# A chunked-attention and gated-FFN kernel: its hand-written order and its engine letters replaced by another set

## The chip, the cores and the metric

The kernel runs on one core of a Trainium2 chip. The metric is device time in microseconds (us) of one execution, on the core that ends last (here the only one). Smaller is better.

## The reference

Attention in chunks of 32 queries, each with 16 keys to the left, 8 to the right and 8 memory keys, then a feed-forward block with a depthwise convolution that makes its own gate. The sizes are batch 4, 8 heads, 768 tokens, head width 64, so a model width of 512, and an inner width of 1024. All inputs but q, k, v and the memory come as float64 words.

```python
for c in range(nc):                       # 24 chunks of 32 queries
    k_full = concat(mem_k, k[l_start:r_end])      # 16 left, 32, 8 right, 8 memory
    scores = scale * q_c @ k_full.T
    a = exp(scores - max); a = a / (sum(a) + 1e-9)
    out[c] = a @ v_full
x = out as (B, S, 512)
h = maximum(x @ w_in, 0)                  # (B, S, 1024)
conv = sum_k conv_w[k] * shift(h, k)      # 3 taps over the tokens
y = (h * sigmoid(conv)) @ w_out
```

## The kernel before

The work is cut into 1309 small operations, each a Python closure that emits a few instructions. A plan records, for each, which tiles it reads and writes; `Plan.run` then emits them in the sequence of the table `ORDER` (lines 35 to 91). Each engine (PE, DVE, ACT, POOL) and the queue of the loads (SP) executes its own instructions strictly in that sequence, so a waiting instruction holds back all behind it on its engine. Strings of letters choose an engine or a variant for each piece: `SOFT` the softmax of a step, `NORM` the engine of its division, `W_IN` and `W_OUT` the way a float64 weight block is taken apart, `TAP`, `MULT` and `LO` the engines of the gate.

The text uses these names for the operations:

- **Steps 0 to 31** are pieces of the attention: one batch, one half of the tokens, two heads each; steps 0 to 3 are done one at a time, later ones in pairs named by the first. qN, kN and vN are the three loads of step N (line 301; on SP, 192, 252 and 384 KB). **S N** is the scores of step N on PE (line 310: 48 weight loads and 48 matmuls in the trace); **T N** the transposes of its probabilities (line 325); **V N** the product with v (line 334).
- The softmax between S and T: maximum (DVE, line 267), then for letter V a subtraction on DVE (line 269) and one exponential on ACT (line 270), for letter A a scaling of the maximum by a negative number on DVE (line 272) and on ACT, straight from PSUM, one exponential for each of 6 (single step) or 12 (pair) slices (line 283); then the sum (290), the reciprocal (293) and the division (294, on DVE or POOL). The score tile `s` is there once: S of the next step waits until the softmax has read it.
- After T, ACT copies the transposed tile (`w_t`, 327), V runs, ACT rounds its result (`x_hi`, 340) and DVE takes the rest (`x_lo`, 341). The tile `t` is there once as well, so the next T waits for that `x_lo`.
- **in0 to in7, out0 to out7** are the loads of the float64 blocks of w_in and w_out (line 208, 512 KB each) and the DVE, ACT and POOL operations that split each into two fp32r parts (lines 212 to 238).
- **F** is a group of three matmuls of 128x384 (line 358), one block of w_in times one quarter of x; **O** a group of three of 128x512 (line 402) for the output. In the whole program there are 256 F, 200 O, 32 S, 18 T and 18 V.

SP's loads go through eight lanes: a load's issue waits until the load eight places ahead of it has landed, and, where its buffer is in use, for the engine that still reads it.

```python
W_IN, W_OUT = ('CSSRMSCr', 'CMCRRSRM')
SOFT = 'VVVVVAAVVAVBVVVBVBVVVAVVVVAVVBAA'
...
            assert after <= done, i
...
        e = Tile('e', lambda: e_of[len(plan.rings['e'][1]) % len(e_of)])
...
    plan.run(ORDER)
```

Of the kernel before, what the change touches and what calls it, by code (L numbers as in the profile page):

```python
# [24 lines left out]
W_IN, W_OUT = ('CSSRMSCr', 'CMCRRSRM')  # L25
TAP = 'AAAAAAAAVAVAVVVAVAVAVVAAVVAAVVAV'
MULT = 'VVVGVVGVVVVVGGGVGVVVVGVVVGGGVVVV'
LO = 'VVVVGGGVVVVVVVVVGVVVGVVVVGVVGVGV'
SOFT = 'VVVVVAAVVAVBVVVBVBVVVAVVVVAVVBAA'
NORM = 'GGVGGGVVGGGGGVGGVVGGVVVVVVVGVGVG'  # L30
# [71 lines left out]
class Plan:  # L102

    def __init__(self):
        self.ops, self.last, self.readers = ([], {}, defaultdict(list))
        self.rings, self.parts = ({}, defaultdict(list))
# [434 lines left out]
```

## Time and profile before

| | |
|---|---|
| median of 3 runs | 353.03 us (352.73 to 353.37) |
| the profiled execution | 352.37 us |
| its span | 350.6 us |
| instructions | 10290 |
| PE, DVE, ACT, POOL busy | 334.1, 233.1, 191.9, 83.6 us |
| HBM read, written | 35.55 MB, 6.29 MB |

The span runs from the first to the last recorded instruction; 1.77 us of the profiled execution's time lie around it. Busy times of different engines overlap, so they do not add up to the span. A busy PE is not a PE at its peak: matmul records overlap one another, and where the next one starts tells the pace better than how long one lasts.

### The profile page before, as it was taken

The page shows a single profiled execution, that of the slowest core. Times are in us where ns is not written, and L with a number is a line of the kernel's source. Part 1 is how long each engine was busy: PE and PEld are TensorE (multiplying, and loading weights), DVE is VectorE, ACT ScalarE, POOL GpSimd, SP SyncE. Part 2 cuts the span into 40 slices and gives each one's busy share as a digit, 9 for nine tenths or more (in the row PEclk, how much of TensorE's full clock was granted, in tenths as well). Part 3 has the DMA queues.
Part 4 walks back from the last instruction along what each step waited for, and adds up shares of the span by engine and source line. Part 5 has one row for each costly group of instructions (what it writes and reads, how often), then busy time and mean ns, then how long its engine had stood idle before and what let it go on. Part 6 is the DMA issues. An engine that isn't in the chain of part 4 may idle for free.

```text
span 350.6 us, 10290 instructions
## 1 busy us (share of the span) xinstructions
PE 334.1 (95%) x4536; PEld 297.1 (85%) x4536; DVE 233.1 (66%) x325; ACT 191.9 (55%) x314; POOL 83.6 (24%) x127
## 2 busy tenths in 40 slices
PE   1589999999999999999999999999999999999996
PEld 0468999989999998887888999998888988998885
DVE  4977998999989997989974143286840332678300
ACT  4434785877687869379842323456743352545311
POOL 1464245124473154111020000402200012121200
PEclk9999999999999999999999999999999999999999
DMA  7966979667677244022401600001212000100022
GB/s 261 391 216 204 314 249 333 230 208 228 200 206 251 66 154 148 27 93 75 125 20 36 243 0 32 0 2 60 65 45 93 30 1 2 60 0 2 0 105 76
DMA packets 19916, 42.49 MB, mean 121 GB/s; under 512 B 2336, under 2 KB 10784, under 8 KB 19872
## 3 DMA queue, kind: packets, MB, share of 16 engines
q1 hardware_dynamic: 19872, 41.85, 35.6%
q8 instruction: 35, 0.57, 0.7%
q14 instruction: 9, 0.07, 0.1%
HBM read 35.55 MB, written 6.29 MB: 119 GB/s over the span
## 4 chain that ended last, share of the span: by engine, by line
PE 85%; DVE 9%; DMA 3%; issue 1%; ACT 0%; POOL 0%; DVEq 0%; ACTq 0%; POOLq 0%
PE f L402 38%; PE f L358 34%; PE t L334 6%; PE s L310 4%; PE t L325 3%; DMA w<-in_w_out_dram 2%; DVE c L378 1%; DMA w<-in_w_in_dram 1%; DVE w_top L217 1%; DVE e L269 1%; DVE top L267 1%; DVE w_top L214 1%; DVE w L223 1%; DVE w_top L216 1%; DVE w L221 1%
## 5 line engine op out<-in xcount | busy, mean ns | idle before, releaser
L402 PE MATMUL f<-w_out_hi,g 128*128 128x512 f32 (+1 forms) x400 | 127.3, 387 | 0.0
L358 PE MATMUL f<-x_hi,w_in_hi 128*128 128x384 f32 x256 | 90.3, 353 | 0.0
L402 PEld LDWEIGHTS f<-w_out_hi,g 128*128 128x128 f32 x400 | 74.1, 188 | 15.2 <-ACT o_sb L405 0.2
L358 PE MATMUL f<-x_lo,w_in_hi 128*128 128x384 f32 x256 | 86.7, 339 | 0.0
L358 PE MATMUL f<-x_hi,w_in_lo 128*128 128x384 f32 x256 | 86.7, 339 | 0.0
L402 PE MATMUL f<-w_out_lo,g 128*128 128x512 f32 (+1 forms) x200 | 77.0, 385 | 0.0
L378 DVE SCALAR_TENSOR_TENSOR c<-h,cw,c 128x768 f32<-128x768 f32 x48 | 49.2, 1044 | 18.6 <-ACT c L374 17.4
L358 PEld LDWEIGHTS f<-x_hi,w_in_hi 128*128 128x128 f32 x256 | 48.6, 190 | 2.7 <-issue 0.2
L358 PEld LDWEIGHTS f<-x_hi,w_in_lo 128*128 128x128 f32 x256 | 48.8, 190 | 1.0
L358 PEld LDWEIGHTS f<-x_lo,w_in_hi 128*128 128x128 f32 x256 | 48.5, 190 | 0.0
L402 PEld LDWEIGHTS f<-w_out_lo,g 128*128 128x128 f32 x200 | 37.6, 188 | 6.6
L405 ACT COPY o_sb<-f 128x512 f32<-128x512 f32 (+1 forms) x25 | 14.2, 573 | 43.4 <-PE f L402 41.3
L379 ACT ACTIVATE c<-c 128x768 f32<-128x768 f32 x32 | 26.9, 847 | 19.6 <-DVE c L378 19.5
L366 ACT ACTIVATE h<-f 128x384 f32<-128x384 f32 x48 | 22.6, 490 | 26.3 <-PE f L358 26.3
L388 POOL TENSOR_TENSOR g<-c,g 128x768 fp32r<-128x768 f32 x8 | 15.4, 1925 | 70.9 <-PE f L402 35.2
L334 PEld LDWEIGHTS t<-w_t,v_t 64*64 64x64 f32 x1536 | 25.2, 140 | 4.6 <-issue 3.3
L334 PE MATMUL t<-w_t,v_t 64*64 64x32 f32 x1536 | 27.2, 224 | 0.1
L387 ACT CAST g<-c 128x768 fp32r<-128x768 f32 x24 | 19.8, 833 | 12.6 <-POOL c L381 7.1
L376 DVE TENSOR_SCALAR c<-h,cw 128x768 f32<-128x768 f32 x14 | 8.6, 617 | 26.3 <-ACT h L366 23.6
L388 DVE TENSOR_TENSOR g<-c,g 128x768 fp32r<-128x768 f32 x16 | 17.3, 1086 | 11.2 <-ACT g L387 11.0
L381 POOL TENSOR_TENSOR c<-c,h 128x768 f32<-128x768 f32 x5 | 8.9, 1781 | 63.4 <-ACT c L379 63.4
L341 DVE TENSOR_TENSOR x_lo<-t,x_hi 128x768 fp32r<-128x768 f32 (+1 forms) x18 | 15.5, 859 | 12.6 <-ACT x_hi L340 12.6
(68 smaller groups left out, 408.5 us busy)
## 6 DMA issues: line engine op xcount, KB each, us to landing
v_t<-in_v_dram SPq DMA_DIRECT2D x32, 384.0 KB, 4.4
k_t<-in_k_dram SPq DMA_DIRECT2D x28, 252.0 KB, 3.9
out_dram<-o_sb SPq DMA_DIRECT2D x23, 256.0 KB, 2.0
q_d<-in_q_dram SPq DMA_DIRECT2D x28, 192.0 KB, 4.4
w<-in_w_in_dram SPq DMA_DIRECT2D x8, 512.0 KB, 6.2
w<-in_w_out_dram SPq DMA_DIRECT2D x8, 512.0 KB, 5.3
h<-in_k_dram SPq DMA_DIRECT2D x4, 252.0 KB, 6.1
h<-in_q_dram SPq DMA_DIRECT2D x4, 192.0 KB, 5.8
```

Source lines behind the costliest of these rows:

```text
L310: nc.tensor.matmul(s.t[w * CH:(w + 1) * CH, h ^ w & 1, (i * NG + g) * KW:(i * NG + g + 1) * KW], lhsT=q_d.t[r, c], rhs=k_t.t[r, c * STEP:c ...
L325: nc.tensor.transpose(out=t.t[:, j, g * P:(g + 1) * P], in_=e.t[:, i, 1:1 + 2 * KW], identity=ident)
L334: nc.tensor.matmul(t.t[h * D:(h + 1) * D, c & 1, c // 2 * CH:(c // 2 + 1) * CH], lhsT=vs[i].t[r, o], rhs=w_t.t[r, i, o], start=True, stop= ...
L341: plan.op(lambda: nc.vector.tensor_tensor(out=lo(), in0=sums(), in1=hi().bitcast(F32), op=ALU.subtract), (t, *keys(x_hi)), keys(x_lo))
L358: nc.tensor.matmul(f.t[:, :TW], lhsT=w_in_p[c][:, fc, cc], rhs=x_p[a].t[:, cc], start=cc == 0 and i == 0, stop=cc == NCC - 1 and i == 2)
L366: nc.scalar.activation(h.t[:, 1 + o:1 + o + TW], f.t[:, :TW], AF.Relu)
L378: plan.op(lambda i=i: nc.vector.scalar_tensor_tensor(out=c.t, in0=h.t[:, i:i + S], scalar=w[i], in1=c.t, op0=ALU.mult, op1=ALU.add), (*H, ...
L379: plan.op(lambda: nc.scalar.activation(c.t, c.t, AF.Sigmoid), (c,), (c,))
L387: plan.op(lambda: nc.scalar.copy(out=g_hi(), in_=x()), (h,), (p[0],))
L388: plan.op(lambda: (nc.vector if lo == 'V' else nc.gpsimd).tensor_tensor(out=g_lo(), in0=x(), in1=g_hi().bitcast(F32), op=ALU.subtract), (h ...
L402: nc.tensor.matmul(ps.t[:, :n], lhsT=g[fc][a].t[:, tt * P:(tt + 1) * P], rhs=w_out_p[c][:, fc, o:o + n], start=fc == 0 and i == 0, stop=fc ...
L405: plan.op(lambda: nc.scalar.copy(out=o_sb.t[:, :n], in_=ps.t[:, :n]), (ps,), (o_sb,))
```

## The change

The table `ORDER` is replaced as a whole (1308 entries now), with the letters that go with it. The way the two probability buffers `e` are handed out is changed too: no longer in turn, but whichever has been given back first; and the check that a ring has a free buffer counts the buffers in use.

```diff
-W_IN, W_OUT = ('CSSRMSCr', 'CMCRRSRM')
-TAP = 'AAAAAAAAVAVAVVVAVAVAVVAAVVAAVVAV'
-MULT = 'VVVGVVGVVVVVGGGVGVVVVGVVVGGGVVVV'
-LO = 'VVVVGGGVVVVVVVVVGVVVGVVVVGVVGVGV'
-SOFT = 'VVVVVAAVVAVBVVVBVBVVVAVVVVAVVBAA'
-NORM = 'GGVGGGVVGGGGGVGGVVGGVVVVVVVGVGVG'
+W_IN, W_OUT = ('CSSSCRmR', 'SMCSRRSC')
+TAP = 'AAAAAAAAAAAVVAAVVVAAVVVAAAAAAAVV'
+MULT = 'VVVGGVVVVGGVGGVGGVVVGGVGGVGGGGVV'
+LO = 'VVVVVVVVVVVVVVGGGGGGVGVVVGGGVVGG'
+SOFT = 'AAVVVAVVVAABAVVBVBVVVAVVVVVVVBVA'
+NORM = 'GGVGGGGVVGGGVVVGGVGGVVVVGVGGGGGG'
 ORDER = (
-    64, 65, 1, 0, 3, 75, 17, 16, 85, 70, 33, 32, 66, 67, 18, 68, 69, 2, 71, 72, 73, 74, 4, 76, 190, 49, 5, 6, 19, 77,
+    64, 0, 1, 75, 16, 17, 85, 70, 65, 33, 71, 48, 2, 66, 73, 67, 68, 72, 69, 32, 3, 74, 4, 18, 76, 5, 49, 6, 77, 95,
...
-                    assert len(used) < size or not used[-size].left, i
+                    assert sum((y.left > 0 for y in used)) < size, i
...
             do()
+            for x in tiles:
+                if not x.left and x.ring in self.freed:
+                    self.freed[x.ring].append(x.t)
...
+    plan.ring('e', len(e_of))
+    plan.freed['e'] = e_of
...
-        plan.ring('e', len(e_of))
-        e = Tile('e', lambda: e_of[len(plan.rings['e'][1]) % len(e_of)])
+        e = Tile('e', lambda: plan.freed['e'].pop(0))
```

Four lines are added ahead of these pieces, so a line of the new kernel has a number larger by 3 to 5 than before (line 310 is 314 now, 358 is 362). In both orders in0 is the first load. The program has as many S, T, V, F and O as before.

**SP, the loads 10 to 22.** Before, in this sequence: v1 and v0, q4, k3, q5, q3, q6, k4, in3, k5, v3 and v2, in4, k6.

```order
L301 DMA v_t<-in_v_dram 128x768 x2
L301 DMA q_d<-in_q_dram 128x384
L301 DMA h<-in_k_dram 128x504
L301 DMA q_d<-in_q_dram 128x384
L301 DMA h<-in_q_dram 128x384
L301 DMA q_d<-in_q_dram 128x384
L301 DMA k_t<-in_k_dram 128x504
L208 DMA w_228<-in_w_in_dram 128x1024
L301 DMA k_t<-in_k_dram 128x504
L301 DMA v_t<-in_v_dram 128x768 x2
L208 DMA w_353<-in_w_in_dram 128x1024
L301 DMA k_t<-in_k_dram 128x504
```

Now, behind q3 and v0: q2, v1, k3, in3, v2, k5, v3, q5 and q4, k4, q6, v5, in4.

```order
L305 DMA h<-in_q_dram 128x384
L305 DMA v_t<-in_v_dram 128x768
L305 DMA h<-in_k_dram 128x504
L213 DMA w_154<-in_w_in_dram 128x1024
L305 DMA v_t<-in_v_dram 128x768
L305 DMA k_t<-in_k_dram 128x504
L305 DMA v_t<-in_v_dram 128x768
L305 DMA q_d<-in_q_dram 128x384 x2
L305 DMA k_t<-in_k_dram 128x504
L305 DMA q_d<-in_q_dram 128x384
L305 DMA v_t<-in_v_dram 128x768
L213 DMA w_368<-in_w_in_dram 128x1024
```

in3 and two of the large v loads have moved ahead of the q and k of step 4; in4 stands behind v5, whose buffer is free only after V1, where before it stood behind a v that waits for V0.

**PE, from S3 on.** Before: S3, V1, the first F, S5 and S4 together, the second F, T2.

```order
L310 MATMUL s<-h 32x64 x24
L334 MATMUL t<-w_t,v_t 64x32 x24
L358 MATMUL f<-x_hi_270,w_in_hi 128x384
L358 MATMUL f<-x_hi_270,w_in_lo 128x384
L358 MATMUL f<-x_lo_273,w_in_hi 128x384
L310 MATMUL s<-k_t,q_d 32x64 x48
L358 MATMUL f<-x_hi_270,w_in_hi 128x384
L358 MATMUL f<-x_hi_270,w_in_lo 128x384
L358 MATMUL f<-x_lo_273,w_in_hi 128x384
L325 MATMUL t<-ident,e_71 128x128 x3
```

Now: S3, V1, the first F, S4, the second F, T2, S5, V2.

```order
L314 MATMUL s<-h 32x64 x24
L338 MATMUL t<-w_t,v_t 64x32 x24
L362 MATMUL f<-x_hi_274,w_in_hi 128x384
L362 MATMUL f<-x_hi_274,w_in_lo 128x384
L362 MATMUL f<-x_lo_282,w_in_hi 128x384
L314 MATMUL s<-k_t,q_d 32x64 x24
L362 MATMUL f<-x_hi_274,w_in_hi 128x384
L362 MATMUL f<-x_hi_274,w_in_lo 128x384
L362 MATMUL f<-x_lo_282,w_in_hi 128x384
L329 MATMUL t<-ident,e_71 128x128 x3
L314 MATMUL s<-k_t,q_d 32x64 x24
L338 MATMUL t<-w_t,v_t 64x32 x24
```

S5 has moved behind the second F and T2; up to and with the first F, PE's sequence is the same as before.

**ACT, the softmax of steps 0 and 1.** Before, after the first weight operation (w_80, w_113 and w_119 are in0, in1 and in2; e_71 and e_73 the two probability buffers):

```order
L227 ACTIVATE w_80<-w_80 128x512
L212 ACTIVATE w_top<-w_113 128x512
L270 ACTIVATE e_71<-e_71 128x3x128
L212 ACTIVATE w_top<-w_119 128x512
L270 ACTIVATE e_73<-e_73 128x3x128
L327 COPY w_t<-t 128x384
```

Now (w_86 and w_92 are in1 and in2):

```order
L224 CAST w_in_hi<-w_top 128x512
L217 ACTIVATE w_top<-w_86 128x512
L287 ACTIVATE e_71<-s,top 128x64 x6
L217 ACTIVATE w_top<-w_92 128x512
L287 ACTIVATE e_73<-s,top 128x64 x6
L331 COPY w_t<-t 128x384
```

Each of the two single exponentials has become six that read the scores themselves.

## Rows read from the trace of the kernel before

**Rows 1.** The page, part 1: busy us, share of the span and instructions of each engine.

```profile
PE 334.1 (95%) x4536; PEld 297.1 (85%) x4536; DVE 233.1 (66%) x325; ACT 191.9 (55%) x314; POOL 83.6 (24%) x127
```

**Rows 2.** The waits of PE over the whole span: who waited, for what, us in total, how often, the longest.

```profile
PE s L310 <- DMA h<-in_q_dram: 8.3, 2, 6.8
PE s L310 <- issue: 1.5, 1, 1.5
PE t L325 <- DVE x_lo L341: 0.2, 1, 0.2
```

**Rows 3.** The chain of work that ended last, in order of time: start, us, engine and line. "issue" is time in which the engine waited for nothing that the profile shows.

```profile
18.94 1.43 PE t L334 x48
20.37 1.26 PE f L358 x3
21.63 0.90 PE s L310 x47
22.53 1.51 issue
24.04 0.96 PE s L310 x47
25.00 1.26 PE f L358 x3
26.25 0.64 PE t L325 x3
...
71.33 0.85 PE t L325 x6
...
347.49 0.37 ACT o_sb L405
```

**Rows 4.** The timeline of the opening: start, us, engine, line, operation, tiles and shapes, count, and in brackets the idle time before it with what ended it. The two PEld rows are weight loads of S3 and of S5 with the first of S4.

```profile
7.84 0.56 DVE L267 TENSOR_REDUCE top<-s 128x6 f32<-128x384 f32 x1
8.51 0.56 DVE L269 TENSOR_TENSOR e<-s,top 128x384 f32<-128x384 f32 x1
9.30 0.96 PE L310 MATMUL s<-h 64*32 64x64 f32 x48 [1.50 <-DMA h<-in_q_dram]
18.27 0.42 PEld L310 LDWEIGHTS s<-h 64*32 64x32 f32 x26 [0.20 <-issue]
20.78 0.52 PE L358 MATMUL f<-x_hi,w_in_lo 128*128 128x384 f32 x1
21.10 0.52 PE L358 MATMUL f<-x_lo,w_in_hi 128*128 128x384 f32 x1
21.55 0.75 PEld L310 LDWEIGHTS s<-k_t,q_d 64*32 64x32 f32 x49 [0.44 <-issue]
27.96 0.34 PE L358 MATMUL f<-x_hi,w_in_lo 128*128 128x384 f32 x1
28.14 0.34 PE L358 MATMUL f<-x_lo,w_in_hi 128*128 128x384 f32 x1
28.41 0.90 PE L334 MATMUL t<-w_t,v_t 64*64 64x32 f32 x48
35.41 2.56 ACT L283 ACTIVATE e<-s,top 128x64 f32<-128x64 f32 x12
```

**Rows 5.** The timeline of SP's issues: start, us of the issue, line, tile and tensor. In turn q5, q3, in4 and k6.

```profile
9.18 0.33 SPq L301 DMA_DIRECT2D q_d<-in_q_dram  x1
10.50 0.33 SPq L301 DMA_DIRECT2D h<-in_q_dram  x1
15.77 1.44 SPq L208 DMA_DIRECT2D w<-in_w_in_dram  x1
22.56 0.33 SPq L301 DMA_DIRECT2D k_t<-in_k_dram  x1
```

**Rows 6.** The DMA queues in the stretch from 15.6 to 15.8 us: packets, MB, share of 16 engines. The instruction queue has no packet between 10 and 15.6 us.

```profile
q8 instruction: 1, 0.02, 33.1%
```

**Rows 7.** The same from 21.6 to 21.8 us; the instruction queue's second packet. The second row is the queue of the loads.

```profile
q8 instruction: 1, 0.02, 34.2%
q1 hardware_dynamic: 3, 0.00, 5.5%
```

**Rows 8.** The page, part 6: DMA issues by tensor: count, KB each, median us to landing.

```profile
v_t<-in_v_dram SPq DMA_DIRECT2D x32, 384.0 KB, 4.4
k_t<-in_k_dram SPq DMA_DIRECT2D x28, 252.0 KB, 3.9
q_d<-in_q_dram SPq DMA_DIRECT2D x28, 192.0 KB, 4.4
w<-in_w_in_dram SPq DMA_DIRECT2D x8, 512.0 KB, 6.2
```

**Rows 9.** Stretches of the opening: us, then busy us and count of PE, PEld, DVE, ACT, POOL, the granted TensorE clock, the DMA share and GB/s.

```profile
20.00:24.00 4.00, 2.53 (x67) 1.80 (x63) 3.19 (x8) 1.87 (x4) 2.45 (x2) 1.00 0.40 122
28.00:30.00 2.00, 2.00 (x55) 1.71 (x54) 0.66 (x3) 0.67 (x3) 0.83 (x1) 1.00 0.56 213
```

**Rows 10.** The timeline around T6 (the PE row): the x_lo that T6 waits for, a POOL operation of a lower-case weight block, and, from 33 us, a division of a pair of steps on POOL.

```profile
33.31 1.47 POOL L294 TENSOR_TENSOR e<-e,z 128x768 f32<-128x768 f32 x1 [0.83 <-PE t L325]
...
45.37 0.95 DVE L341 TENSOR_TENSOR x_lo<-t,x_hi 128x768 fp32r<-128x768 f32 x1
...
45.88 1.55 POOL L214 TENSOR_SCALAR w_top<-w_top 128x536 f32<-128x536 f32 x1 [2.10 <-ACT w_top L212]
...
47.21 0.88 PE L325 MATMUL t<-ident,e 128*128 128x128 f32 x6
```

More of the change, by code (lines that the diff above doesn't have):

```diff
@@ L105, in __init__ @@
         self.ops, self.last, self.readers = ([], {}, defaultdict(list))
-        self.rings, self.parts = ({}, defaultdict(list))
+        self.rings, self.parts, self.freed = ({}, defaultdict(list), {})
     def ring(self, name, n):
```

118 rows, old and new, of the table ORDER are left out of this document.

## The prediction, as it went on record

> **What bounds the kernel now.** I read the page first: PE is busy for 95% of the span [rows 1], so only what PE waits for, or the pace at which it works, can move the end. Next the waits of PE: over the whole span 8.3 us for the first q loads, 1.5 us for "issue", 0.2 us for an x_lo, and some 3 us for two divisions in the opening (the first three of these are in [rows 2]). Then the chain in order of time: from 24.04 us it is PE work with one stop at 71.33, and the last PE work ends at 347.49, where ACT takes the last tile [rows 3]. Everything that is to change the time by more than a few tenths must therefore lie before 25 us, or be a new wait behind it. Both orders hold the same PE work, so I work out when PE has done the same pieces in both, and carry the difference to the end.
>
> **The two stops for "issue".** PE stands still in S3 after 22 of its 48 weight loads, until 18.27, and in S4 after the first one, from 22.53 to 24.04 [rows 3, 4]. Between the two stops it took 52 instructions of S3, 96 of V1, 6 of F, 96 of S5 and one of S4: 251. Counting about as many back from the first stop (44 of S3, 6, 96, 96 and 6 of T1, V0, S2, T0) leads to the last instructions of S1, which ends at 9.30 + 0.96 = 10.26 [rows 4]. The instruction queue moves one packet of 0.02 MB from 15.7 us and the next from 21.7 [rows 6, 7]; PE goes on 2.6 and 2.3 us after. I read this so: PE's instructions come in blocks of about 251 of those I count, the fetch of the block after next is asked for when PE enters a block (10.3 and 18.3 us), and it runs only when the loads issued until then have landed. That fits: the last load issued before 10.3 is q5 at 9.18, and in4, which waits for q5's lane, is issued at 15.77 [rows 5]; and at 21.7 the queue of the loads is as good as empty, 5.5% against the fetch's 34.2% [rows 7].
>
> The Trainium skill (Runtime: NRT & Kernel Launch, "Instruction fetch mechanics") describes the fetch in blocks of 256 instructions and calls the cost of crossing a block mostly hidden. The trace disagrees for this opening: 1.51 us at one crossing.
>
> **The change, step by step.**
>
> 1. *The softmax of steps 0 and 1.* Before, the score tile is free for S1 after the maximum and the subtraction, at 8.51 + 0.56 = 9.07, and S1 starts at 9.30 [rows 4]. Now it is free after a scaling and six exponentials on ACT; twelve took 2.56 us [rows 4], so six take 1.28. The maximum ends at 8.40, the scaling takes about 0.2 (an estimate, under the half of a subtraction), so the exponentials run from about 8.7 to 10.0, S1 from 10.05 to 11.0: 0.75 later.
> 2. *The first fetch.* It is now asked for at 11.0. The release that let q3 go at 10.50 (in2 has landed, eight places ahead of it) now lets v2 go; k5 waits for k2, 252 KB behind in2, so until about 11.2. So the fetch stands behind v2. By the sizes of the loads [rows 8], v2 is the end of 4976 KB, and q5 before was the end of 4272. Between 10.5 (in2, 2424 KB) and 15.7 the queue moved 1848 KB, 355 KB a us. The 704 KB more are 1.98 us: fetch at 17.7, PE past the place in S3 at 17.7 + 2.5 = 20.2, where it was 18.27. That is 1.9 us lost. It covers the later T1, which costs nothing of its own: the exponentials of step 1 end at about 13.4, behind them come the copy for V0, S2 and V0 (to 15.95), then x_hi and x_lo, so T1 runs from 17.5 to 18.35, and S3 would be at its 22nd weight load at 18.8.
> 3. *The second fetch.* It is asked for at 20.2. By then the loads up to q6 are out, 6440 KB; v5 waits for V1 and in4 stands behind it, so both come later. Before, 6952 KB had landed by 21.7. 512 KB fewer at 355 KB a us are 1.4 us: the fetch runs at once or by 20.5, PE could go on by 22.9, and needs the block only at its second F, at 24.5. The stop of 1.51 us goes.
> 4. *PE from there.* With the rows of before [rows 3]: rest of S3 0.67, V1 1.43, F 1.26, S4 0.90: 24.46. Second F 1.26: 25.72. T2 0.64: 26.36. S5 0.96: 27.32. Before, the same pieces were done at 26.25 + 0.64 = 26.89. PE is 0.43 us behind.
> 5. *The pace of PE.* The granted clock reads 1.00 in all stretches [rows 9], but the second and third matmuls of an F start 0.32 us apart at 21 us and 0.18 apart at 28 [rows 4]: 384 columns at 1.2 GHz, then near 2.4 GHz. The higher level came at 27.96. If it comes at the same time now, what lies before it at the low level after 26.89 shrinks from 1.07 us to 0.64 us; the half of the difference, 0.21, is won.
> 6. *The stop at 71.33.* That T waited 0.24 us for an x_lo [rows 2, 3]. DVE's queue up to the same x_lo loses two subtractions and two operations of the gate of about 0.9 us and gains small ones, some 3.6 us in all, while PE comes to that T 2.6 us of work earlier; with 1 us more room the wait should go: 0.24 won.
>
> All else I cost at nothing: in the middle part POOL gets more divisions and products, but PE's work covers them there (POOL is busy for 24% [rows 1]). Both orders end in O of half width, ACT's copy of the last half tile and its store, so the 3.1 us from PE's last matmul to the end of the span, 350.6 − 347.49, stay [rows 3]. If that cover fails, the price is rival D's. The wait I look for next is T6's.
>
> Sum: +0.43 (step 4, which holds steps 1 to 3) − 0.21 − 0.24 = 0.0 against the profiled 352.37. That run stands 0.66 under the median of 353.03, so the median to expect is **353.0 us**. A change under 0.2% (0.7 us) is one that this measurement can't tell from none.
>
> **Rivals.**
>
> - *A, faster: the fetch comes ahead of v2.* If PE asks for the block some tenths before S1's last instruction, v2 (issued at 10.5) stands behind it. Then 384 KB at 355 are 1.1 us less in step 2: 351.9. For it: 11.0 and 10.5 are close. Against: PE's entry is counted from rows that put it at S1's end. 22%.
> - *B, faster: loads do not hold a fetch.* Then PE isn't held in S3 at all, it passes the place at about 18.8 with T1's delay, 1.4 us sooner than in step 2: 351.6. Against: the two packets that ran 5 and 3 us after PE entered a block. 8%. The Trainium skill (DMA: Bandwidth & Descriptors, "Queues, rings and completion order") has each DMA engine go round its queues packet by packet, by which B would hold; the late packets speak against it here [rows 6, 7].
> - *C, slower: PE's pace rises later.* Before, the level rose 3.9 us after the stop, and PE had done S4, F, T2 and most of another F. The long work before that stop, from 16.8 to 22.5, with one F in it, left the level low [rows 4]. Now S5 and V2 stand behind the second F. If the level rises only in the F that follow V2, at about 31 us, then V2 takes 1.5 us where my case has about 1.2 (1.43 and 0.90 were a V at the two levels [rows 3, 4]), and from 28.8 to 31 F run at half the pace: 0.3 + 1.1 = 1.4 us more, 354.4. It decides from the point where F rows behind V2 still start 0.32 apart. For it: less F in that stretch; against: PE now has no stop from 20.2 on. 21%.
> - *D, slower: T6 waits for POOL.* T6 now takes its division from POOL (1.47 us for a pair), behind a lower-case weight operation of 1.55 us; before, T6 started 0.9 us after its x_lo had ended [rows 10]. I find the division's end within 0.2 us of T6; in full it costs 1 us: 354.0. 6%.
> - *E, slower: the change doesn't do what I read in it, and the second fetch still stops PE.* If the loads drain 1.5 us later than in step 3, PE waits up to 0.8 us at its second F: 353.8. 3%.
>
> **How the numbers follow.** My case, 0.0 within 0.7 us, has 40%. A and B make 30% for faster, C, D and E 30% for slower. The range reaches from below B (351.6) to just over C (354.4): 351.4 to 354.7; its ends take in a fetch that is 0.7 us later (behind k5, 252 KB) together with one of the small waits, and leave out A and C in sum with others. My case's own range is 352.3 to 353.7.
>
> **What would show it.** In the profile of the changed kernel: S1's start near 10.05; the first packet of the instruction queue at 17.7, the second before 21.5; PE's wait for "issue" in S3 until 20.2 and none at the second F; the end of S5 (now its own piece) at 27.3; the spacing of the F rows from 28.8 on; no wait at T6. I am wrong if PE's last O ends more than 0.7 us from 347.5, and the step at fault is the first of these places that is off by so much.

## The result: 355.96 us, 1.1% slower than before, outside the range

The changed kernel takes 355.96 us (median of 5 runs, 354.67 to 357.16 and one of 360.37), the kernel before 353.03. The ratio is 1.0106, with a 95% interval of 1.0083 to 1.0129. The profiled execution took 355.96 us, with a span of 354.0. Measured again later beside other kernels, the same program gave 1.0059 (1.0028 to 1.0090), with runs from 352.47 to 356.44. An execution of each measurement was profiled, one of 355.96 us and one of 352.64, and what differs between them is part of the answer.

The page, part 1, of the changed kernel (columns as in [rows 1]):

```profile
PE 334.6 (95%) x4536; PEld 297.5 (84%) x4536; DVE 221.8 (63%) x307; ACT 195.3 (55%) x316; POOL 109.4 (31%) x141
```

PE has as much work as before. The waits of PE (who, for what, us in total, how often, the longest):

```profile
PE s L314 <- ACT e L287: 3.2, 2, 2.6
PE t L338 <- issue: 2.5, 1, 2.5
PE t L329 <- DVE e L290: 2.4, 1, 2.4
```

The 1.5 us for "issue" and the 0.2 us for an x_lo of [rows 2] are gone. A new wait for "issue" of 2.5 us stands in a V, where before there was none. PE's timeline in the opening (S1, T1, S3, the second F, S5, and the first F behind V2):

```profile
10.29 0.97 PE L314 MATMUL s<-h 64*32 64x64 f32 x48 [2.63 <-ACT e L287]
18.90 0.88 PE L329 MATMUL t<-ident,e 128*128 128x128 f32 x3 [2.38 <-DVE e L290]
19.71 0.97 PE L314 MATMUL s<-h 64*32 64x64 f32 x48
24.20 0.69 PE L362 MATMUL f<-x_hi,w_in_hi 128*128 128x384 f32 x1
24.70 0.69 PE L362 MATMUL f<-x_hi,w_in_lo 128*128 128x384 f32 x1
25.18 0.53 PE L362 MATMUL f<-x_lo,w_in_hi 128*128 128x384 f32 x1
26.19 0.72 PE L314 MATMUL s<-k_t,q_d 64*32 64x64 f32 x48
28.00 0.33 PE L362 MATMUL f<-x_hi,w_in_lo 128*128 128x384 f32 x1
28.17 0.34 PE L362 MATMUL f<-x_lo,w_in_hi 128*128 128x384 f32 x1
```

S5 ends at 26.9, as the same pieces did before [rows 3], and the F rows are 0.17 us apart by then. Nothing is lost in the opening. PE's timeline at the loss (S7, which is the second half of S6; V4; S9 and S8; an F):

```profile
34.11 0.73 PE L314 MATMUL s<-k_t,q_d 64*32 64x64 f32 x48
...
38.25 1.48 PE L338 MATMUL t<-w_t,v_t 64*64 64x32 f32 x87
42.23 0.36 PE L338 MATMUL t<-w_t,v_t 64*64 64x32 f32 x9 [2.51 <-issue]
42.52 1.45 PE L314 MATMUL s<-k_t,q_d 64*32 64x64 f32 x96
43.90 0.69 PE L362 MATMUL f<-x_hi,w_in_hi 128*128 128x384 f32 x1
44.38 0.52 PE L362 MATMUL f<-x_hi,w_in_lo 128*128 128x384 f32 x1
44.70 0.52 PE L362 MATMUL f<-x_lo,w_in_hi 128*128 128x384 f32 x1
```

PE stands still in V4 after 87 of its 96 matmuls, and behind the stop the F rows are 0.32 us apart again. Stretches around it (us, then busy us and count of PE, PEld, DVE, ACT, POOL, the granted clock, DMA share, GB/s):

```profile
36.00:39.60 3.60, 3.60 (x101) 3.35 (x99) 3.56 (x7) 2.57 (x5) 2.33 (x4) 1.00 1.01 318
39.80:42.20 2.40, 0.00 (x0) 0.00 (x0) 1.77 (x4) 1.35 (x2) 2.40 (x7) 1.00 0.84 327
42.20:44.00 1.80, 1.77 (x106) 1.56 (x106) 0.00 (x0) 1.38 (x3) 0.43 (x1) 0.76 0.09 27
44.00:46.00 2.00, 2.00 (x7) 2.00 (x8) 1.99 (x4) 1.20 (x2) 1.49 (x1) 0.50 0.56 115
46.00:48.00 2.00, 2.00 (x12) 2.00 (x11) 2.00 (x3) 0.85 (x1) 1.60 (x5) 0.87 0.91 325
```

The DMA engines are full until the stop, and the granted clock is 0.76, 0.50 and 0.87 behind it: 0.24 x 1.8 + 0.50 x 2 + 0.13 x 2 = 1.7 us of PE's time at the full clock. Stop and clock together are 4.2 us. PE's last work ends 3.4 us later than before (350.82 against 347.42), so some 0.8 us were won elsewhere.

The stop is a fetch. The DMA queues from 40.0 to 40.1 us (packets, MB, share):

```profile
q1 hardware_dynamic: 12, 0.04, 94.3%
q8 instruction: 1, 0.02, 62.0%
```

PE goes on 2.2 us after this packet. SP's issues ahead of it (start, us, line, tile and tensor): k9, the convolution's weights, in6, q8, k8, v6, in7.

```profile
33.58 0.38 SPq L305 DMA_DIRECT2D k_t<-in_k_dram  x1
34.00 0.43 SPq L215 DMA_DIRECT2D w<-in_conv_w_dram  x1
34.53 0.38 SPq L213 DMA_DIRECT2D w<-in_w_in_dram  x1
35.02 0.36 SPq L305 DMA_DIRECT2D q_d<-in_q_dram  x1
35.43 0.42 SPq L305 DMA_DIRECT2D k_t<-in_k_dram  x1
35.91 0.42 SPq L305 DMA_DIRECT2D v_t<-in_v_dram  x1
36.38 0.43 SPq L213 DMA_DIRECT2D w<-in_w_in_dram  x1
```

PE's blocks hold 254 of its weight loads and matmuls here (the prediction counted 251). Counted back from V4's 87th matmul (174 instructions of V4, 24 of four F, 12 of T4, 6 of an F, 38 of S7) the border before lies after the 29th weight load of S7, and in two kernels below PE is seen to stop just there. PE passed it at 34.4, and the packet for the block behind V4's 87th came 5.6 us later. All stops for "issue" that are told of below lie at such borders, but for one that is named.

### The profile page after: what moved, and what is told of

Read it like the earlier page. It is cut to its first block, busy times and chain, and to the rows that moved or that the text cites. A ratio compares the mean times of both kernels' runs of the same rounds, so it can differ in the third digit from the quotient of the medians.

```text
span 354.0 us, 10293 instructions
## 1 busy us (share of the span) xinstructions
PE 334.6 (95%) x4536; PEld 297.5 (84%) x4536; DVE 221.8 (63%) x307; ACT 195.3 (55%) x316; POOL 109.4 (31%) x141
## 4 chain that ended last, share of the span: by engine, by line
PE 92%; DVE 3%; DMA 2%; issue 1%; ACT 1%; SPq 0%; DVEq 0%; ACTq 0%
PE f L362 39%; PE f L406 37%; PE t L338 7%; PE s L314 5%; PE t L329 3%; DMA w<-in_w_in_dram 2%; DVE c L382 1%; DVE w L229 0%; DVE w_top L222 0%; DVE z L294 0%; ACT o_sb L409 0%; ACT c L378 0%; DVE top L271 0%; SPq L305 0%; DVE w_top L219 0%
## 5 line engine op out<-in xcount | busy, mean ns | idle before, releaser
L382 DVE SCALAR_TENSOR_TENSOR c<-h,cw,c 128x768 f32<-128x768 f32 x48 | 51.4, 1091 | 15.0 <-ACT c L378 13.6
L370 ACT ACTIVATE h<-f 128x384 f32<-128x384 f32 x48 | 23.0, 490 | 32.9 <-PE f L362 32.8
L409 ACT COPY o_sb<-f 128x512 f32<-128x512 f32 (+1 forms) x25 | 14.0, 567 | 44.3 <-PE f L406 34.3
L385 POOL TENSOR_TENSOR c<-c,h 128x768 f32<-128x768 f32 x9 | 14.6, 1618 | 68.6 <-ACT c L383 62.7
L392 POOL TENSOR_TENSOR g<-c,g 128x768 fp32r<-128x768 f32 x10 | 19.4, 1948 | 37.1 <-ACT g L391 37.1
L392 DVE TENSOR_TENSOR g<-c,g 128x768 fp32r<-128x768 f32 x14 | 15.2, 1100 | 20.3 <-ACT g L391 20.3
L380 DVE TENSOR_SCALAR c<-h,cw 128x768 f32<-128x768 f32 x10 | 7.8, 783 | 27.0 <-ACT h L370 27.0
L298 POOL TENSOR_TENSOR e<-e,z 128x768 f32<-128x768 f32 (+1 forms) x12 | 17.7, 1479 | 19.1 <-DVE z L297 17.4
```

The lines of the kernel that those rows point to most:

```text
L298: plan.op(lambda: (nc.vector if norm == 'V' else nc.gpsimd).tensor_tensor(out=keep()[:, :N], in0=keep()[:, :N], in1=z.t[:, :N].unsqueeze(3 ...
L370: nc.scalar.activation(h.t[:, 1 + o:1 + o + TW], f.t[:, :TW], AF.Relu)
L382: plan.op(lambda i=i: nc.vector.scalar_tensor_tensor(out=c.t, in0=h.t[:, i:i + S], scalar=w[i], in1=c.t, op0=ALU.mult, op1=ALU.add), (*H, ...
L385: plan.op(lambda: (nc.vector if mult == 'V' else nc.gpsimd).tensor_tensor(out=y(), in0=c.t, in1=h.t[:, 1:S + 1], op=ALU.mult), (c, h), (h ...
L392: plan.op(lambda: (nc.vector if lo == 'V' else nc.gpsimd).tensor_tensor(out=g_lo(), in0=x(), in1=g_hi().bitcast(F32), op=ALU.subtract), (h ...
L409: plan.op(lambda: nc.scalar.copy(out=o_sb.t[:, :n], in_=ps.t[:, :n]), (ps,), (o_sb,))
```

## The experiments

The edits that move something use one helper, at the end of the file:

```diff
+def moved(order, ops, behind):
+    rest = [i for i in order if i not in ops]
+    at = rest.index(behind) + 1
+    return (*rest[:at], *ops, *rest[at:])
```

The numbers are operations. They are the loads 106 in4 (of the kernel before), 116 in5, 127 in6, 137 in7, 138 the convolution's weights, 192 v4, 211 k6 (before), 212 v6, 214 q7, 271 k8, 290 q10, 294 q11; on PE 217 is S7 and 162 the F behind it; on ACT 117 is in5's first operation.

**First set: which loads hold the fetch?** Theory Q: those issued up to the request. Theory S: all that are under way.

```diff
+ORDER = moved(ORDER, (212,), 290)
...
-        plan.op(lambda: nc.sync.dma_start(out=w.t[:, :n].rearrange('p n w -> p (n w)'), in_=src.bitcast(U32)), w=((w, 2),))
+        def bring():
+            cols = 64 if key == 'in7' else n
+            nc.sync.dma_start(out=w.t[:, :cols].rearrange('p n w -> p (n w)'), in_=src.bitcast(U32)[:, :2 * cols])
+            if cols < n:
+                nc.gpsimd.memset(w.t[:, cols:n].bitcast(F32), 0.0)
+        plan.op(bring, w=((w, 2),))
```

> The changed kernel, with the loads that are issued just behind PE's request for the block taken away from the stretch 36 to 43 us: v6 is issued only behind q10, and of in7 one eighth is loaded (the rest of its buffer is set to zero by POOL; this part of the computation is left out). 832 KB fewer stand beside the fetch. Theory Q (the fetch waits for the loads that were issued before PE asked for the block, up to k8 at 35.4, and for no others): packet still at about 40.0, PE's stop in V4 still 2.3 to 2.7 us, time 355.5 to 356.5. Theory S (the fetch shares the DMA engines with all loads under way, and gets through when the jam thins): the jam ends about 2 us sooner, stop 0.3 to 1.2 us, time 352 to 354.5.

Measured: runs of 353.83 to 358.99, ratio 1.0114 (1.0048 to 1.0179). In the profile (358.99) there is no stop in V4; the packet comes 2.8 us behind the border. The time was lost elsewhere: S4 started 1.2 us late, at 24.48 (its k4 landed at 24.34, in the changed kernel at 22.64), PE's pace rose only at 34.1 instead of 26.1, and V6 stopped for 2.26 us. The late pace is what rival C had described. PE came to the border in S7 at 38.2 instead of 34.3, so the run does not decide between Q and S.

The same edit with 'in6' in place of 'in7', and no moved load:

> The changed kernel, with only one eighth of in6 loaded (the rest of its buffer is set to zero by POOL; this part of the computation is left out). in6 is issued at 34.5, before the request. 448 KB fewer at some 370 KB a us stand ahead of the fetch. Theory Q: packet 1.2 us earlier, at 38.8, stop in V4 1.3 us, time 1.2 to 2.8 us shorter than 355.96 (the more, the less the granted clock falls after a shorter stop): 353.1 to 354.8. Theory S: the same direction but less than with 832 KB fewer in the other kernel, stop about 2 us. If the stop is no fetch: no change.

Measured: 353.34, packet at 35.4, 1.7 us behind the border, no stop in V4 and no fall of the clock there (V6 stops for 0.76 us). The wait is 3.9 us shorter than in the profile of the changed kernel, where theory Q had put 1.2. It is not the 448 KB alone: an execution of the unedited program has 3.0 (fourth set), and against that one it is 1.3.

```diff
         def turn():
+            for i in range(40 if cc == 2 and x_hi is x_of[0, 0][0] else 0):
+                nc.tensor.matmul(t.t[:32, 0, :32], lhsT=ident[:, :32], rhs=ident[:, :32], start=True, stop=True)
             for i in range(N):
```

> The changed kernel with 40 small matmuls more (32x32 from the identity, overwritten by T2) ahead of T2 on PE: 80 instructions more, so that every later block of PE's instructions begins 80 instructions earlier in the program, at an unchanged stream of loads. The block that held up V4 is then asked for before S6, at about 32 us, when in6, q8 and k8 are not issued yet. Theories Q and S: no stop in V4, no fall of the granted clock behind it: 4.1 us won, some 0.6 lost to the added matmuls, 352.4 (351.9 to 353.0), if no later border meets another jam. If the stop belongs to V4 or to the loads alone and not to the place of a block's border: the stop stays, 356.5.

Measured: 360.63, the slowest. The 40 matmuls of the code are 80 weight loads and 80 matmuls in the trace (4616 of each instead of 4536), so the borders moved by 160 instructions and not by the 80 that were expected. V4 has no stop, as expected, but the border behind it, now sooner as well, fell into S8 after 38 of its 96 matmuls, and PE stopped there for 2.81 us. Between these two borders stand only matmuls of V4 and S8: 1.85 us of work, less than the 2.2 us from a packet to its use. I had followed one border only.

```diff
+ORDER = moved(ORDER, (212, 127, 137), 138)
```

> The changed kernel with SP's order behind the load of the convolution's weights turned round: v6, in6, in7 ahead of q8, k8 (in6, q8, k8, v6, in7 before). The same loads, the same bytes in the stretch; ahead of PE's request now stand v6, in6 and in7 (1408 KB) where in6, q8 and k8 (956 KB) stood. Theory Q: 452 KB more at 370 KB a us, packet 1.2 us later, at 41.2, stop 3.7 us, time 357.2 (356.8 to 358.2 with the clock low for longer). Theory S: the jam is the same, packet at about 40, time 355.5 to 356.5.

Measured: 357.59; packet at 41.0, 5.8 us behind the border (5.6 in the changed kernel), stop 2.93 us. Theory Q's 1.2 us more did not come; the fetch went ahead of q8 and k8, the last loads now.

**Second set: can the stop be taken away?** In turn:

```diff
+ORDER = moved(ORDER, (127,), 294)
```

> The changed kernel with in6 issued ahead of v4 instead of behind the convolution's weights; nothing else moves. Between 32 and 34.5 us the DMA engines have room (60 to 300 KB a us against 370 when full), so some 400 KB of the loads that keep them full until 41 us run ahead of PE's request. Theory (a fetch waits while the loads keep the DMA engines full): the jam is shorter by about 1.1 us, stop in V4 1.4 instead of 2.5 us, time 354.0 (353.0 to 355.0; the lower end if the granted clock does not fall behind the shorter stop). If the wait of the fetch does not depend on these loads: 2.5 us, 356.

Measured: 358.26; the wait grew to 6.7 us and the stop to 3.75. Here PE is seen held at the border in S7 (weight loads of S7: start, us, count):

```profile
34.37 0.28 PEld L314 LDWEIGHTS s<-k_t,q_d 64*32 64x32 f32 x29 [0.25 <-issue]
34.84 0.25 PEld L314 LDWEIGHTS s<-k_t,q_d 64*32 64x32 f32 x19 [0.19 <-issue]
```

```diff
+ORDER = moved(ORDER, (212,), 290)
```

> The changed kernel with v6 issued behind q10 instead of ahead of in7, so behind the first matmuls of S9 and past the jam; nothing else moves and all of every load is taken. 384 KB fewer stand in the jam, but they were issued at 35.9, 1.5 us after PE entered the block. If loads that are issued after the request hold the fetch too: stop 1.5 us or less, 353 to 354.5. If only loads issued up to the request count: stop 2.5 us, time 356.

> The changed kernel with both moves, in6 ahead of v4 and v6 behind q10. Theory: wait of the fetch 5.7 minus 1.1 minus up to 1.0, stop in V4 0.4 us or none, no fall of the granted clock: 352.2 (351.5 to 353.2), level with the kernel before or 0.8 better. If neither load matters: 356.

The second of these has both lines. Measured: 357.18 and 357.51. Both lost the stop in V4 (0.2 us and none; packets 3.0 and 2.8 us behind the border), and both got one of 1.99 us in V6, with a fall of the clock behind it, and a wait for a k (0.6 and 1.0 us). The stop was gone in one place and there in another.

```diff
-SOFT = 'AAVVVAVVVAABAVVBVBVVVAVVVVVVVBVA'
+SOFT = 'VVVVVAVVVAABAVVBVBVVVAVVVVVVVBVA'
```

> The changed kernel with the softmax of steps 0 and 1 undone (SOFT of these two back to V: subtraction on DVE and one exponential on ACT). S1 starts at about 9.4 instead of 10.3, the first packet of the instruction queue comes at 15.5 to 16.4, T1 up to 0.8 us sooner, S5 ends 0 to 0.8 us sooner. If the opening decides the result: 355.2. If it doesn't, because the collision of fetch and loads in V4 goes with PE's place and shifts as a whole: 355.5 to 356.5, with the stop of about 2.5 us in V4 still there.

Measured: five runs of 351.58 to 352.83 and five of 355.81 to 356.79, none between. The profile is of the first group (S3's two parts, S5):

```profile
18.21 0.64 PE L314 MATMUL s<-h 64*32 64x64 f32 x21
19.19 0.66 PE L314 MATMUL s<-h 64*32 64x64 f32 x27 [0.34 <-issue]
24.99 0.72 PE L314 MATMUL s<-k_t,q_d 64*32 64x64 f32 x48
```

PE is 1.2 us sooner in S5, although S3 now waits for the first fetch. In V4 it has no stop: the packet came 1.8 us behind the border. So the opening is worth about 1.2 us in this execution. What the 4 us between the groups are is not shown, as no run of the second group was profiled. Only two of its five runs have a mean granted clock below 1.00 (0.995 and 0.990; one stretch of 3.4 us at 0.50 makes 0.995 of a run), so in the other three it is not a stop with a fall of the clock behind it.

**Third set: theory M against theory J.** In the profiles so far with a long wait (the changed kernel, heavy loads first, in6 early), PE had been held at the border in S7; in those with a short one it had not. In the changed kernel the hold is too short for a row of its own. Weight loads in the 0.16 us around the border, of the changed kernel:

```profile
34.27:34.43 0.16, 0.12 (x17) 1.00 0.89 192
```

and of the same program in an execution without the long wait (the fourth set):

```profile
33.67:33.83 0.16, 0.16 (x31) 1.00 0.24 96
```

17 loads and a gap against 31 and none. Theory M: a block that PE has to wait for makes the next request late. Theory J: the fetch just waits for the jam to end.

```diff
+ORDER = moved(ORDER, (217,), 162)
```

> The changed kernel with the scores of step 7 (the second half of S6) behind the next F instead of ahead of it. PE then enters the block ahead of V4's about 0.5 us later, so that this block has been there for some 0.5 us, where PE came to its border 0.1 us too soon in the changed kernel. Theory M (a block that PE has to wait for, if only for 0.1 us, makes the next request some 1.5 us late, which puts it behind in6, q8 and k8): no such wait at the border in S7, packet for V4's block at 36 to 38.5 us, stop in V4 0 to 1.1 us, time 351.8 to 354.3. Theory J (the fetch only waits for the jam to end): packet at 40, stop 2.2 to 3, and 0.5 us less time in V4's block: time 356 to 357.

Measured: 353.7 (eight of ten runs from 353.16 to 354.17). PE is not held in S7, the packet comes 3.0 us behind the border, the stop in V4 is 0.44 us, and the clock does not fall there. V6 stops for 1.97 us in the profiled run of 356.5, and S4 waits for its k there as in the first experiment:

```profile
24.50 0.96 PE L314 MATMUL s<-k_t,q_d 64*32 64x64 f32 x48 [1.11 <-DMA k_t<-in_k_dram]
```

This is a second way in which the new order of the loads can cost time, without a fall of the clock. In the kernel before, k4 landed at 17.94 and k5 at 19.77, and S5 and S4 began at 21.6; in the changed kernel k4 lands at 22.64, 0.7 us ahead of S4.

```diff
+ORDER = moved(ORDER, (217,), 162)
+ORDER = moved(ORDER, (127,), 271)
```

> The changed kernel with S7 behind the next F, as in the kernel with that alone, and in6 issued behind k8 instead of ahead of q8. Theory M: the request for V4's block is in line ahead of in6, packet at 35.5 to 37, no stop in V4, no fall of the granted clock there: 351.9 (351.3 to 353.0). Theory J: the same bytes in the jam, packet at 40, stop 2 to 3 us: 355.5 to 357.

Measured: 354.42. Packet at 36.5, 1.2 us behind the border, no stop (theory J's 40 us is out). But in6, now later, costs 1.0 us at an F and 0.26 at T6 (PE's timeline: V4, S8 and S9, the F and T6):

```profile
38.74 1.60 PE L338 MATMUL t<-w_t,v_t 64*64 64x32 f32 x96
40.27 1.24 PE L314 MATMUL s<-k_t,q_d 64*32 64x64 f32 x96
45.67 0.44 PE L362 MATMUL f<-x_lo,w_in_hi 128*128 128x384 f32 x1 [0.99 <-DVE x_lo L345]
47.43 0.77 PE L329 MATMUL t<-ident,e 128*128 128x128 f32 x5 [0.26 <-POOL e L298]
```

With the edit of SOFT added:

> The changed kernel with S7 behind the next F, in6 behind k8, and the softmax of steps 0 and 1 as before (letter V). Alone, the softmax gave times about 352 without and about 356 with a stop in V4 (ten runs in two groups). Theory M: one group only, 351.5 (350.8 to 352.5), the best of all. Theory J: two groups as before, median 352 to 356.

Measured: 353.64, runs from 352.73 to 356.21, with the same two waits; not one group.

The kernel before, with its stop of 1.51 us [rows 3] attacked:

```diff
+ORDER = moved(ORDER, (106,), 211)
```

> The kernel before with in4 issued behind k6 instead of ahead of it, that is after V1's buffer is free, and no longer ahead of the second fetch: 512 KB fewer in line, 1.4 us. Both theories: second packet at 20.0 to 20.5 instead of 21.7, the stop of 1.51 us in S4 is 0 to 0.3 us, time 351.0 (350.3 to 352.0) against 352.4 to 353.0. If the stop in S4 is no fetch or not held by in4: no change.

Measured: the second packet at 19.7 instead of 21.6, and S5 and S4 run without a stop (one row):

```profile
21.62 1.62 PE L310 MATMUL s<-k_t,q_d 64*32 64x64 f32 x96
```

The profiled run took 350.13, but the eight runs behind the ratio go from 350.13 to 354.72, ratio 0.9993 (0.9965 to 1.0021). The stop was a fetch behind in4; that this version is faster isn't shown. Its profiled run is the fastest here.

**Fourth set: is it the hold, or in6's place (theory P)?**

```diff
+ORDER = moved(ORDER, (127,), 271)
```

> The changed kernel with in6 issued behind k8, and PE's order as in the changed kernel (S7 ahead of the next F). Theory M (a block that PE has to wait for makes the next request late): PE comes to the border in S7 0.1 to 0.25 us too soon, the next packet stands behind q8, k8 and in6 as before and comes 4.5 to 6 us after that, stop in V4 of 2 to 3 us with a fall of the granted clock, 355.5 to 357. Should PE by chance not have to wait at the border in S7, then also no long wait behind it. Theory P (in6's place decides): packet at 36 to 37.5, stop 0 to 0.3 us, 351.9 to 353, whatever happens at the border in S7.

Measured: 354.46. By chance PE was not held in S7; packet 1.7 us behind the border, no stop, and in6's two waits again. This tells nothing between M and P.

> The changed kernel, nothing edited. Theory M: if PE has to wait at the border in S7 (0.05 to 0.3 us), the packet for V4's block comes more than 4.5 us later and PE stops in V4 for 2 to 3 us; if it doesn't have to, the packet comes within 3.1 us and there is no stop over 0.3 us, with a time of 352 to 353.5. Without theory M the two need not go together.

Measured: the profiled run took 352.64. PE is not held in S7, the packet comes at 36.7, 3.0 us behind the border, and V4 runs through; S8 then waits 1.0 us for its k (S7, V4, S9, S8):

```profile
33.56 0.72 PE L314 MATMUL s<-k_t,q_d 64*32 64x64 f32 x48
...
37.69 1.65 PE L338 MATMUL t<-w_t,v_t 64*64 64x32 f32 x96
39.28 0.72 PE L314 MATMUL s<-k_t,q_d 64*32 64x64 f32 x48
41.00 0.71 PE L314 MATMUL s<-k_t,q_d 64*32 64x64 f32 x48 [1.00 <-DMA k_t<-in_k_dram]
```

Of these ten runs only one (356.44) has a mean granted clock of 0.995; in the first measurement of the changed kernel four of five have 0.994 or 0.995. The ten still have a median of 354.19, against 352.05 for the kernel before beside them. So the stop with its fall of the clock fits the times of the first measurement, of which one execution was profiled; what most of these ten lost without a fall of the clock is not shown.

**Fifth set: the hold made certain, and made impossible.** The first line is the one kernel, the other two the other.

```diff
+ORDER = moved(ORDER, (192,), 214)
```

```diff
+ORDER = moved(ORDER, (116,), 294)
+ORDER = moved(ORDER, (117,), 114)
```

> The changed kernel with v4 issued ahead of the q of steps 9 and 11 (at about 29 us instead of 32): 384 KB more in line ahead of the fetch of S7's block, packet 0.5 to 1 us later, PE always has to wait at the border in S7, by 0.3 to 1.2 us. Theory M: the request behind it is late in every run, the packet for V4's block comes more than 4.5 us after PE has passed the border, PE stops in V4 for 1.5 us or more, and the times form one group at 356 to 358.5. Without theory M: the load is only moved out of the later jam, V4's fetch waits 1 us less than 5.7 us or not at all, and times are 353 to 355.5.

Measured: 355.7 (353.45 to 357.21). PE is held in S7 for 1.42 us, and yet the next packet comes 2.4 us after that and V4 stops for 0.18 us only (S7's parts, V4's end):

```profile
33.90 0.44 PE L314 MATMUL s<-k_t,q_d 64*32 64x64 f32 x29
35.76 0.41 PE L314 MATMUL s<-k_t,q_d 64*32 64x64 f32 x19 [1.42 <-issue]
...
41.22 0.36 PE L338 MATMUL t<-w_t,v_t 64*64 64x32 f32 x9 [0.18 <-issue]
```

Theory M as I had put it falls: a hold alone does not make the long wait. What differs is SP: here q8 was issued at 36.22, so that between 32.8 and 36.2 no load was issued, where the changed kernel issued five from 34.53 on.

> The changed kernel with in5 issued behind the q of step 11 (at about 32 us instead of 27.4), with its first operation on ACT moved behind the x_hi of step 3: 512 KB fewer ahead of the fetch of S7's block, and as many more in the jam behind it. Theory M: packet for S7's block at about 31.0 to 31.7, PE never has to wait at the border in S7, the next request is in time and ahead of in6, packet at 35.5 to 37.5, no stop over 0.3 us in V4 and no fall of the granted clock there, one group of times at 352 to 354 (ACT and DVE get in5's block some 2 us later, which may cost up to 1 us). Theory J (the fetch waits for the loads of the jam): 512 KB more, stop in V4 of 3 to 4 us, 356 to 358.

Measured: 356.8. PE is not held in S7, the packet comes 2.9 us behind the border, V4 has no stop by the fetch; that part is theory M's and not J's. But ACT waited 3.87 us for in5, and V4 for ACT (ACT's operation on in5, then V4):

```profile
36.89 0.66 ACT L217 ACTIVATE w_top<-w 128x512 f32<-128x512 f32 x1 [3.87 <-DMA w<-in_w_in_dram]
...
39.23 1.60 PE L338 MATMUL t<-w_t,v_t 64*64 64x32 f32 x96 [1.43 <-ACT w_t L331]
```

S8 then stopped for 1.8 us (at no border; the scores' tile was not free, since DVE too had waited for in5) and V6 for 1.42. I had put in5's delay at up to 1 us.

**All profiles on one line each** (us; the border is the one in S7):

| kernel | held there | border to packet | stop in V4 |
|---|---|---|---|
| changed | 0.15 | 5.6 | 2.51 |
| heavy first | 0.15 | 5.8 | 2.93 |
| in6 early | 0.30 | 6.7 | 3.75 |
| v4 early | 1.42 | 2.4 | 0.18 |
| eleven others with this border | none | 1.0 to 3.0 | 0 to 0.44 |

The holds are the distances between the starts of two weight loads, which are at most 0.06 elsewhere in S7 of these kernels; for v4 early it is the row's. Unheld, the packet went ahead of every load that was issued more than about 0.6 us behind the border. After the three short holds it went behind loads that were issued up to 0.7 to 1.8 us behind it. (Where it stood in the line is worked out from the bytes that had been moved when its packet ran.) SP issues a load of 192 to 512 KB every 0.45 us in that stretch, and the DMA engines move some 320 KB a us, so a request that comes 1 us later in the line waits some 2.5 us longer (an estimate).

Shown is: the stop is the fetch; its wait hangs on the loads that are issued around the moment when PE passes the border before; the same program runs with and without it. Open is why a hold of 0.15 us puts the request so far back in the line (a hold of 1.42 us put it back by 0.5 to 0.8), and so whether the hold or something that goes with it is the cause.

One thing in the traces bears on this, and no run tests it. Counted on to the end with PE's semaphore instructions, 256 to a block, the changed kernel has 35 borders behind the start, as many as packets, and the stops in S3, S7, V4 and V6 all stand on one. Among short matmuls (V and S), with the DMA engines idle, the packet runs 0.7 to 1.1 us behind the moment at which PE passes the border before, and 1.4 us behind it in V4, where PE had just been held. Among the long matmuls of F and O it runs ahead of that moment, by up to 4.3 us (packet at 323.8, border at 328.1). So the request goes out before PE itself is at the border, the earlier the longer the matmuls there last. F stand ahead of S7: a PE that is held may lose that lead, and its request would then come behind more loads.

## Why the prediction was wrong

1. *Softmax of steps 0 and 1.* S1 started at 10.29, forecast 10.05. Right; the scaling took 0.43 us, where 0.2 was estimated.
2. *First fetch.* Packet at 16.4, not 17.7, and no stop in S3. v2 landed only at 17.36, so the fetch did not wait for it, as rival A had held. PE came late for another reason: T1 at 18.90 instead of 17.5. T1 needs the x_lo of step 0, and in the new order that stands on DVE behind a weight operation (two DVE rows; before, it began at 16.06):

```profile
16.80 1.49 DVE L229 TENSOR_SCALAR w<-w_top 128x512 uint32<-128x512 uint32 x1
18.21 0.55 DVE L345 TENSOR_TENSOR x_lo<-t,x_hi 128x384 fp32r<-128x384 f32 x1
```

The page of the profile puts this wait of T1 down to the short DVE operation on `e` that ends 0.04 us after the x_lo; the probabilities that T1 reads had been ready at 16.8. PE passed the place in S3 at 19.9, forecast 20.2. The number came out nearly right by luck, the reason was wrong.

3. *Second fetch.* Packet at 22.25, not by 20.5, and the second F lost 0.2 us: its rows are 0.50 and 0.48 us apart, those of an F before 0.48 and 0.32. The stop of 1.51 us went, as forecast. (The two packets before ran at 15.78 and 21.60, and PE went on 2.5 and 2.4 us after them, not 2.6 and 2.3.)
4. *PE's sum.* S5 ended at 26.9, forecast 27.3, before 26.89: 0.4 us better.
5. *Pace.* It rose at about 26 us, before at 27.96: more than the 0.21 us was won. Rival C did not come here; it did in the profile of the first experiment.
6. *The stop at 71.33* went. T6 did not wait for POOL (rival D).
7. *"All else I cost at nothing"* is the step that failed, with its reason that PE's work covers the middle part. A fetch is not covered by PE's work: it must arrive within the block before it. I followed two fetches and stopped at 25 us, though the rule that I had read off the first two applied to every one behind them. Rival E named the mechanism, at the wrong border and at 0.8 us; it cost 2.5, and 1.7 more by the clock.

The order of the loads is what changed. One stretch, 30.5 to 32 us, before:

```profile
30.50:32.00 1.50, 1.50 (x54) 1.41 (x54) 1.40 (x4) 0.61 (x2) 0.81 (x1) 1.00 0.00 0
```

and in the changed kernel:

```profile
30.50:32.00 1.50, 1.50 (x83) 1.16 (x85) 1.50 (x3) 0.48 (x1) 0.35 (x1) 1.00 1.00 375
```

Before, the DMA engines were idle there, and the fourth packet came at 30.1, 4.3 us ahead of its use. Now they are full, the packet comes at 32.1 and 2.2 us later PE is at the border, to the tenth. The next one then stands in a burst of five loads. The forecast of 353.0 is about what the program took in the profiled execution without the stop (352.64); in the one with it, it took 356.

The Trainium skill (DMA: Bandwidth & Descriptors, "Queues, rings and completion order") lets each DMA engine take its queues in turn, packet by packet. Waits of 5.6 us with the engines full, in which 1.7 MB of loads were moved, speak against that as a bound on a fetch, as the two late packets before had.

## What to carry to other kernels

Where one engine bounds the kernel, list every instruction fetch, not only those that stopped it: mark the borders (here every 252 to 254 weight loads and matmuls of PE), take the time that the block before lasts, and subtract the 2.2 us or more from packet to use; what is left is how long the fetch may stand behind loads. A block of short matmuls (V and S in a row) leaves nothing (1.85 us in the third experiment), so keep bursts of loads away from the moment at which PE enters it. When runs of one program fall into two groups, profile one of each group before you price the change.

## What was not expected of the hardware

- Among short matmuls, a fetch that met idle DMA engines came 0.7 to 1.4 us after PE had entered the block before, one in a burst of loads up to 6.7 us after; among long matmuls with idle DMA engines it came up to 4.3 us ahead of PE. Where PE was held, it went on 2.2 to 2.9 us after the packet.
- After some stops the granted clock was 0.50 for 3.4 us (behind 2.51, 2.93 and 3.75 us in V4, 2.81 in S8, 1.99, 1.64 and 1.42 in V6), after others it did not fall (2.26 and 1.97 us in V6). The length of the stop alone does not decide it.
